# Gated linear attention into a cosine router: products of 64 by 64 on TensorE for scores and state outputs, pairs of outputs in two PSUM banks, a new order of the turnings

## The chip, the cores and the metric

One core of a Trainium2 chip. The metric is the device time of one execution in microseconds (us), the median of three runs; lower is better.

## The reference

Two layers, all in 32-bit floats. The first is a gated linear attention over 4 sequences (batch) of 768 positions, with 8 heads of width 48:

```
f = sigmoid(f_logit)
for t in range(768):
    state = f[t] * state + outer(k[t], v[t])      # one 48 x 48 state per sequence and head
    y[t]  = q[t] @ state
```

The outputs of the 8 heads side by side are 3072 rows x of width 384. The second layer sends each row to one of 8 experts, the one whose embedding is nearest to the row by cosine, and computes `gate * (relu(x @ w1[e]) @ w2[e])`, with w1 of 384 x 1024 and w2 of 1024 x 384.

## The kernel before, in words

The attention runs in 24 **steps**, each a chunk of 128 positions of one sequence (`steps`, L713: six chunks, in each the four sequences in turn). Within a chunk the recurrence is written as products of matrices. For step i:

- `decays` (ACT, L740) and `suffixes` (L748: one product on PE, a clip on DVE at L753, two exponentials on ACT) make the decay factors `ek` and `eq`.
- `keys` and `queries` (DVE, L788 and L799) scale k and q by them; `keys2` and `queries2` turn both on PE (`turn`, L734) and copy the turned tiles out of PSUM as `kz` (ACT) and `qa` (DVE). Two heads, a **pair** (hp), share the 128 partitions of such a tile, the even head in the lower half, the odd in the upper (par 0 and 1), each head padded from 48 to 64 rows.
- `scores` (L810) multiplies kz by qa, one product of 64 rows by 128 columns for each head, into two banks sc0 and sc1; `scores2` masks them on DVE into `am`.
- `whole` and `carry` (POOL, L760 and L769) take the decay of the whole chunk through a small DMA into `pc_all`, and multiply the old state of the sequence by it: `old`. `carried` (L780) copies `old` on ACT into `st`, a tile in which each head has 64 columns over all 128 partitions, zero in the half of the other head.
- `outputs` (L849) adds up for each head, in one bank `f_y`, a product with the old state (L859, 128 rows by 64 columns, `st`; none in the first chunk of a sequence) and one with the masked scores (L865). ACT copies the bank out as `xT` (L870).
- `update2` (L830) makes the new state (L838 on PE, an addition on DVE at L846). `rows_out` (L873) turns the outputs into rows and router logits with one product by `unit` for each pair (L881); `logits`, `route`, `count` and `place` rank the rows by expert, and `scatter` (POOL, L936) sends them to `x_sorted` in DRAM, sorted by expert.

The order of all instructions on each engine is as written. The first steps follow a list (`opening`, L1144), then a loop (L1170) runs for i from 4 to 22; in one turn of it PE gets: suffixes(i+2), keys2(i+1), queries2(i+1), rows_out(i-2), a ranking product in every second to fourth turn (`settle`), scores(i), outputs(i-1), update2(i). The loads of q, k, v and f_logit (L719, DMAs of 192 KB issued by SP) run six steps ahead, from L1171 on; the first expert's weights are issued behind the loads of i = 8. Some straight code then ends the last steps (L1191 to L1213), and starts the first expert with 256 of its rows (L1213 to L1247).

PSUM has eight banks. In the attention stage three are the rotating buffers `tp` (ps_t, taken in turn by suffixes, keys2 and queries2), and misc, small, sc0, sc1 and f_y take one each. The experts follow in a second part (L1250 on), bound by PE throughout, which the change doesn't touch.

Of the kernel before, what the change touches and what calls it, by code (L numbers as in the profile page):

```python
# [10 lines left out]
FP32 = mybir.dt.float32  # L11
# [563 lines left out]
def kernel(  # L575
# [25 lines left out]
    nc = tc.nc  # L601
# [33 lines left out]
    with ExitStack() as fast:  # L635
# [50 lines left out]
            wts[k] = w1, w2  # L686

        with tc.tile_pool(name="f_fix", bufs=1) as fix, tc.tile_pool(name="f_work", bufs=2) as work, tc.tile_pool(
            name="ps_t", bufs=3, space=PSUM
        ) as ps_t, tc.tile_pool(name="ps_s", bufs=1, space=PSUM) as ps_s:  # L690
            NLD = 6
            lds = {nm: [fix.tile([P, H, DH], FP32, name=f"f_{nm}{i}") for i in range(NLD)] for nm in "qkf"}
            NV = NLD + 2
            lds["v"] = [fix.tile([P, H, 64], FP32, name=f"f_v{i}") for i in range(NV)]
            NS = 2
            sts = [fix.tile([P, HP, 2, 64], FP32, name=f"st{i}") for i in range(NS)]
            halves = [slice(0, 64), slice(64, P)]
            misc = ps_s.tile([P, 512], FP32, name="misc")
            small = ps_s.tile([P, 512], FP32, name="small")
# [19 lines left out]
            def load(nm, i):  # L719
# [11 lines left out]
                if nm == "v":  # L731
                    live[i]["v"] = t

            def turn(src, pairs=range(HP)):  # L734
                ps = ps_t.tile([P, HP, P], FP32, name="tp", tag="tp")
                for hp in pairs:
                    nc.tensor.transpose(ps[:, hp], src[:, 2 * hp : 2 * hp + 2].rearrange("p h d -> p (h d)"), ident)  # L737
                return ps
# [8 lines left out]

            def suffixes(i):  # L748
                L = live[i]
                ps = ps_t.tile([P, HP, P], FP32, name="tp", tag="tp").rearrange("p n t -> p (n t)")[:, 0 : H * DH]  # L750
                nc.tensor.matmul(ps, lhsT=upon, rhs=L["lf"], start=True, stop=True)  # L751
                cl = work.tile([P, H * DH], FP32, name="f_cl", bufs=1)
                nc.vector.tensor_scalar(cl, ps, S_MAX, None, ALU.min)  # L753
                ek = work.tile([P, H, DH], FP32, name="f_ek", bufs=3)
                nc.scalar.activation(ek.rearrange("p h d -> p (h d)"), cl, AF.Exp, scale=-1.0)  # L755
                eq = work.tile([P, H, DH], FP32, name="f_eq", bufs=2)
                nc.scalar.activation(eq.rearrange("p h d -> p (h d)"), cl, AF.Exp)
                L["ek"], L["eq"] = ek, eq
# [10 lines left out]
            def carry(i):  # L769

                b, c = steps[i]
                if c == 0:
                    return
                old = work.tile([P, HP, DH], FP32, name="old", bufs=3)
                nc.gpsimd.tensor_tensor(  # L775
                    old, state[b], pc_all[:, i].unsqueeze(2).to_broadcast([P, HP, DH]), ALU.mult
                )
                live[i]["old"] = old

            def carried(i):  # L780
                if steps[i][1] == 0:
                    return
                st = sts[i % NS]
                for par, r in enumerate(halves):
                    nc.scalar.copy(st[r, :, par, 0:DH], live[i]["old"][r])
                live[i]["st"] = st

            def keys(i):  # L788
                L = live[i]
# [20 lines left out]
            def scores(i):  # L810
                L = live[i]
                kz, qa = L["kz"], L["qa"]
                sc = [ps_s.tile([P, HP, P], FP32, name=f"sc{par}") for par in range(2)]
                for hp in range(HP):
                    for par in range(2):
                        r = slice(64 * par, 64 * par + 64)
                        nc.tensor.matmul(sc[par][:, hp], lhsT=kz[r, hp], rhs=qa[r, hp], start=True, stop=True)  # L817
                L["sc"] = sc

            def scores2(i):  # L820
# [28 lines left out]
            def outputs(i):  # L849
                b, c = steps[i]  # L850
                L = live[i]
                if i == NST - 1:
                    y = ps_t.tile([P, HP, P], FP32, name="tp", tag="tp")
                else:
                    y = ps_s.tile([P, HP, P], FP32, name="f_y")
                if c:
                    for hp in range(HP):
                        for par, r in enumerate(halves):
                            nc.tensor.matmul(  # L859
                                y[r, hp], lhsT=L["st"][:, hp, par], rhs=L["qa"][:, hp],  # L860
                                start=hp == 0, stop=False, skip_group_check=True,
                            )
                for hp in range(HP):
                    for par, r in enumerate(halves):
                        nc.tensor.matmul(  # L865
                            y[r, hp], lhsT=L["v"][:, 2 * hp + par], rhs=L["am"][:, par, hp],
                            start=c == 0 and hp == 0, stop=True, skip_group_check=True,
                        )
                xT = work.tile([P, HP, P], FP32, name="f_xT")
                nc.scalar.copy(xT, y)  # L870
                L["xT"] = xT

            def rows_out(i):  # L873
                L = live[i]
                rows_ps = misc
                if i == NST - 1:
                    rows_ps = ps_t.tile([P, HP, P], FP32, name="tp", tag="tp").rearrange("p n t -> p (n t)")
                rows_ps = rows_ps[:, 0 : HP * RW].rearrange("p (n w) -> p n w", w=RW)
                L["rows"] = rows_ps
                for hp in range(HP):  # L880
                    nc.tensor.matmul(rows_ps[:, hp], lhsT=L["xT"][:, hp], rhs=unit[:, hp], start=True, stop=True)  # L881
                x4 = xg[(i // B) % 2]
                row = x4[:, i % B]
                if i % B == 0:
                    nc.scalar.copy(x4[:, :, C_TOK], tok[:, i : i + B])
                x = row[:, 0:D]
                nc.scalar.copy(x.rearrange("p (n w) -> p n w", n=HP), rows_ps[:, :, 0 : 2 * DH])
                sq = work.tile([P, D], FP32, name="f_sq", bufs=1)
                nc.scalar.activation(sq, x, AF.Square, accum_out=row[:, C_SSQ : C_SSQ + 1])
                L["row"] = row  # L890
# [73 lines left out]
            def first():  # L964
# [24 lines left out]
                nc.vector.memset(pc_all, 1.0)  # L989
                for t in lds["v"][1:]:  # L990
                    nc.gpsimd.memset(t[:, :, DH:64], 0.0)
                for t in sts:
                    nc.gpsimd.memset(t, 0.0)
                for t in xg:
                    nc.gpsimd.memset(t[:, :, D:R], 0.0)
# [2 lines left out]
            def norm(part):  # L998
# [3 lines left out]
                    nc.scalar.activation(esq, emb[:, :, 0:DH], AF.Square, accum_out=ss)  # L1002
                if part == 6:
                    for hp in range(HP):
                        nc.scalar.copy(unit[:, hp, 0 : 2 * DH].rearrange("p (r d) -> p r d", r=2), eyes)
                if part == 1:
                    nc.gpsimd.tensor_scalar(ss, ss, 1.0e-30, None, ALU.max)
                    nc.gpsimd.tensor_tensor(rroot, ss, rroot, ALU.pow)
# [13 lines left out]
            def units():  # L1022
                ps = misc[:, 0 : HP * E]
                for hp in range(HP):
                    nc.tensor.transpose(
                        ps[:, hp * E : hp * E + E],
                        emb[:, 2 * hp : 2 * hp + 2].rearrange("e h d -> e (h d)"),
                        ident[0:E, 0:E],
                    )
                nc.scalar.copy(unit[:, :, 2 * DH : RW], ps.rearrange("p (n e) -> p n e", e=E))  # L1030

            def prepare(part):
# [79 lines left out]
            def at(i, fn):  # L1112
                if 0 <= i < NST:
                    fn(i)
# [55 lines left out]
            for i in range(FROM, NST - 1):  # L1170
                loads(i)  # L1171
                at(i + 3, decays)
                at(i + 2, suffixes)
                at(i + 1, carry)
                at(i + 2, whole)
                at(i + 1, keys2)
                at(i + 1, queries2)
                at(i + 2, keys)
                at(i + 2, queries)
                at(i - 2, rows_out)  # L1180
                settle()
                at(i - 2, logits)
                send(1 if i < NST - 4 else 2)
                at(i, scores)
                at(i, scores2)
                at(i, carried)
                at(i - 1, outputs)
                finish(i - 2)
                at(i, update2)
                if i == FROM:  # L1190
                    prepare(2)  # L1191
            scores(NST - 1)
            scores2(NST - 1)
            carried(NST - 1)
            rows_out(NST - 3)
            settle()
            outputs(NST - 2)
# [12 lines left out]
            settle()  # L1210
            finish(NST - 1)
            send(B)
            xt = [ps_t.tile([P, 2, EARLY], FP32, name="tp", tag="tp") for _ in range(2)]  # L1213
            for c in range(DC):
                for j in range(2):
                    nc.tensor.transpose(xt[c // 2][:, c % 2, j * P : j * P + P], xs_a[:, j, c * P : c * P + P], ident)
# [7 lines left out]
            )  # L1224
            whose(1)
            for f in range(FC):
                ps = ps_t.tile([P, 2, EARLY], FP32, name="tp", tag="tp")[:, 0]
                for c in range(DC):
                    nc.tensor.matmul(  # L1229
                        ps, lhsT=wts[0][0][:, c, f * P : f * P + P], rhs=xT_0[:, c, 0:EARLY],  # L1230
# [7 lines left out]
                    check()  # L1238
                if f == 6:
                    checked()  # L1240
                    lt = [ps_t.tile([P, 2, 2, PL], FP32, name="tp", tag="tp", padded_shape=[P, 2, 2, P]) for _ in range(2)]
                    for c in range(DC):
                        for j in range(2):
                            nc.tensor.transpose(lt[c // 2][:, c % 2, j], xs_b[0:PL, j, c * P : c * P + P], ident[0:PL, 0:PL])
# [264 lines left out]
```

## Time and profile before

| what | value |
|---|---|
| median of three runs | 430.54 us (430.49 to 430.96) |
| the profiled execution, its own time | 428.34 us |
| span from its first to its last instruction | 426.6 us |
| PE busy | 417.0 us, 98% of the span |
| ACT, DVE, POOL busy | 46%, 62%, 55% |

The span ends 1.7 us short of the execution's own time. PE is TensorE's products, PEld its weight loads, DVE VectorE, ACT ScalarE, POOL GpSimd, SPq the queue that issues DMAs. Each product of 32-bit floats is two matmul instructions in the trace, so 8 heads are 16 matmuls.

### The profile page before, as it was taken

Reading aid. Unit: us, or ns where it says so; the run is one execution under the profiler, and the core shown is the slowest. Engines: PE = TensorE matmul, PEld = TensorE weight load, DVE = VectorE, ACT = ScalarE, POOL = GpSimd, SP = SyncE. Lnnn points to the kernel's source line nnn. Section 1 sums busy time; section 2 is a strip of 40 time slices with the busy share of each in tenths; the row PEclk is TensorE's granted clock in tenths of the full one; section 3 lists DMA queues with packets and bytes.
Section 4 is the critical chain, followed back from the end, with each engine's and each line's share of the span. In section 5 each row is a group of like instructions: output and inputs, shape, how many; then the busy total and the mean of one; then the engine's idle time right before and its main releaser. Section 6 shows DMA issues by size and latency. Waiting matters only on the chain.

```text
span 426.6 us, 9051 instructions
## 1 busy us (share of the span) xinstructions
PE 417.0 (98%) x3384; PEld 337.6 (79%) x3384; DVE 263.8 (62%) x673; ACT 198.2 (46%) x480; POOL 234.1 (55%) x265
## 2 busy tenths in 40 slices
PE   7999999999999999999999999999999999999994
PEld 5688989898989989659858957966966966967952
DVE  4778776677777434776765584595585585583500
ACT  7888787678776531242062063044134134144210
POOL 8535543564456337606764773886972963962111
PEclk9999999999999999999999999999999999999998
DMA  8999999899931327910380191093083083051011
GB/s 173 188 198 213 243 222 235 287 223 223 219 90 40 120 78 246 320 42 2 124 287 9 14 368 43 2 306 98 20 298 114 2 288 120 2 164 40 19 54 40
DMA packets 120480, 61.60 MB, mean 144 GB/s; under 512 B 104779, under 2 KB 114112, under 8 KB 120428
## 3 DMA queue, kind: packets, MB, share of 16 engines
q1 hardware_dynamic: 113612, 51.21, 45.3%
q0 software_dynamic: 6816, 9.73, 7.0%
q8 instruction: 29, 0.48, 0.5%
q14 instruction: 23, 0.19, 0.1%
HBM read 49.58 MB, written 11.63 MB: 143 GB/s over the span
## 4 chain that ended last, share of the span: by engine, by line
PE 84%; issue 8%; POOL 3%; SPq 2%; DMA 1%; DVE 1%; POOLq 1%; ACT 0%; DVEq 0%
PE h_ps L1311 25%; PE y_ps L1372 20%; PE sc L817 6%; PE f_y L865 5%; PE misc L881 5%; PE f_y L859 5%; PE tp L737 5%; PE tp L751 4%; PE tp L1229 2%; PE small L838 2%; POOL out_dram L1399 2%; PE x_tp L1272 2%; PE y_tp L1412 2%; SPq L730 1%; DMA f_q<-in_q_dram 1%
## 5 line engine op out<-in xcount | busy, mean ns | idle before, releaser
L1311 PE MATMUL h_ps<-xT,w 128*128 128x384 f32 (+6 forms) x384 | 130.8, 484 | 0.0
L1340 POOL TENSOR_TENSOR wsum<-w 128x512 f32<-128x512 f32 x63 | 78.9, 1279 | 53.9 <-PE y_ps L1372 48.8
L1311 PEld LDWEIGHTS h_ps<-xT,w 128*128 128x128 f32 x384 | 68.0, 190 | 38.7 <-issue 24.0
L1318 ACT ACTIVATE hT<-h_ps 128x384 f32<-128x384 f32 (+6 forms) x60 | 29.8, 497 | 129.3 <-PE h_ps L1311 129.3
L1383 DVE TENSOR_TENSOR yTs<-yTs,y_ps 128x147 f32<-128x147 f32 (+6 forms) x189 | 48.5, 296 | 53.8 <-ACT yTs L1385 26.8
L1399 POOL DMA_INDIRECT out_dram<-f_yo,gtok x30 | 42.6, 1420 | 47.1 <-ACT f_yo L1398 43.0
L1372 PE MATMUL y_ps<-hsum,wsum 128*128 128x147 f32 (+5 forms) x384 | 51.1, 283 | 0.0
L1340 DVE TENSOR_TENSOR hsum<-hT 128x588 f32<-128x588 f32 (+6 forms) x49 | 49.0, 1025 | 0.0
L1372 PEld LDWEIGHTS y_ps<-hsum,wsum 128*128 128x128 f32 x384 | 48.3, 189 | 0.0
L937 POOL DMA_INDIRECT x_sorted<-f_xg,f_pos_i x24 | 24.5, 1019 | 18.6 <-DVE hot L914 8.4
L825 DVE TENSOR_TENSOR am<-sc,causal 128x512 f32<-128x512 f32 x48 | 30.8, 683 | 3.9 <-PE sc L817 3.8
L762 POOL COPY f_pc<-f_ek 1x384 f32<-1x384 f32 x24 | 22.4, 934 | 19.5 <-ACT f_ek L755 18.8
L817 PE MATMUL sc<-qa,kz 64*128 64x128 f32 x384 | 27.9, 285 | 0.0
L1273 DVE COPY xT<-x_tp 128x384 f32<-128x384 f32 (+5 forms) x21 | 12.3, 584 | 24.7 <-PE x_tp L1272 24.4
L1385 ACT ACTIVATE yTs<-y_ps 128x147 f32<-128x147 f32 (+6 forms) x63 | 15.0, 286 | 25.6 <-DVE yTs L1383 15.0
L1372 PE MATMUL y_ps<-hT,wsum 128*128 128x147 f32 (+5 forms) x192 | 26.1, 283 | 0.0
L775 POOL TENSOR_TENSOR old<-new,pc_all 128x192 f32<-128x192 f32 x20 | 10.1, 504 | 28.8 <-DMA pc_all<-f_pc 27.5
L1340 POOL TENSOR_TENSOR wsum<-w,wsum 128x512 f32<-128x512 f32 x14 | 20.0, 1425 | 10.7 <-PE y_ps L1372 10.1
L817 PEld LDWEIGHTS sc<-qa,kz 64*128 64x128 f32 x384 | 23.3, 187 | 2.6 <-DVE am L825 0.5
L1372 PEld LDWEIGHTS y_ps<-hT,wsum 128*128 128x128 f32 x192 | 24.3, 189 | 0.0
L865 PE MATMUL f_y<-am,f_v 128*64 128x128 f32 x368 | 24.2, 274 | 0.0
L881 PE MATMUL misc<-unit,f_xT 128*128 128x104 f32 x184 | 24.1, 274 | 0.0
(194 smaller groups left out, 717.1 us busy)
## 6 DMA issues: line engine op xcount, KB each, us to landing
w<-in_moe_w_dram SPq DMA_DIRECT2D x16, 1536.0 KB, 10.7
f_k<-in_k_dram SPq DMA_DIRECT2D x24, 192.0 KB, 4.1
f_q<-in_q_dram SPq DMA_DIRECT2D x24, 192.0 KB, 4.1
f_v<-in_v_dram SPq DMA_DIRECT2D x24, 192.0 KB, 4.0
f_f<-in_f_logit_dram SPq DMA_DIRECT2D x20, 192.0 KB, 4.0
xs<-x_sorted SPq DMA_DIRECT2D x5, 700.0 KB, 9.0
x_sorted<-xs_b SPq DMA_DIRECT2D x1, 1600.0 KB, 8.5
xs<-x_sorted SPq DMA_DIRECT2D x2, 600.0 KB, 7.2
```

Of the source, the lines that this page charges most:

```text
L762: nc.gpsimd.tensor_copy(row[:, :, 0:DH].rearrange("o r d n -> o n r d"), live[i]["ek"][0:1].rearrange("o (n r) d -> o n r d", r=2))
L817: nc.tensor.matmul(sc[par][:, hp], lhsT=kz[r, hp], rhs=qa[r, hp], start=True, stop=True)
L825: nc.vector.tensor_tensor(am[:, par], sc[par], causal.unsqueeze(1).to_broadcast([P, HP, P]), ALU.mult)
L865: nc.tensor.matmul(y[r, hp], lhsT=L["v"][:, 2 * hp + par], rhs=L["am"][:, par, hp], start=c == 0 and hp == 0, stop=True, skip_group_check= ...
L881: nc.tensor.matmul(rows_ps[:, hp], lhsT=L["xT"][:, hp], rhs=unit[:, hp], start=True, stop=True)
L937: nc.gpsimd.indirect_dma_start(out=x_views[s][:], out_offset=bass.IndirectOffsetOnAxis(ap=pos_i[:, s : s + 1], axis=0), in_=live[s]["row"] ...
L1311: nc.tensor.matmul(ps, lhsT=w1[:, c, f * P : f * P + P], rhs=xTs[k][:, c, lo:cap], start=c == 0, stop=c == DC - 1,)
L1318: nc.scalar.activation(hTs[k][:, f, lo:cap], ps, AF.Relu)
L1340: engine.tensor_tensor(blocks[6 + i], blocks[one], blocks[other], ALU.add if sign > 0 else ALU.subtract)
L1372: nc.tensor.matmul(ps, lhsT=h if rows_first else w, rhs=w if rows_first else h, start=m == 0, stop=m == FC // 2 - 1,)
L1383: nc.vector.tensor_tensor(y, y, ps, ALU.add if sign > 0 else ALU.subtract)
L1399: nc.gpsimd.indirect_dma_start(out=out_views[k * NB + j][:], out_offset=bass.IndirectOffsetOnAxis(ap=gtok[0:n, k, j : j + 1], axis=0), in_ ...
```

## The change

It computes the same. Five things change in the attention stage:

1. `scores`: each head's product of 64 rows by 128 columns becomes two of 64 by 64, one for each half of the columns.
2. `outputs`: the product with the old state takes `old` itself (three tiles `olds`, padded to 64 columns), 64 rows by 64 columns, in place of the zero-padded `st`. `carried` and its two ACT copies a step go. The outputs of even pairs lie in bank f_y, those of odd pairs in a new bank f_y_odd, and there with the two heads' halves swapped; `xT` is copied out in two halves. The constants in `unit` are swapped to match.
3. `ps_t` has two buffers in place of three, since f_y_odd takes a bank. Until the first outputs, f_y_odd serves as a third turning bank (`bank`).
4. In the loop keys(i+2) and rows_out(i-2) come ahead of queries2(i+1).
5. At the end of the stage the banks sc0 and sc1 join the rotation.

```
-            name="ps_t", bufs=3, space=PSUM
+            name="ps_t", bufs=2, space=PSUM
...
-            NS = 2
-            sts = [fix.tile([P, HP, 2, 64], FP32, name=f"st{i}") for i in range(NS)]
+            olds = [fix.tile([P, HP, 64], FP32, name=f"old{i}") for i in range(3)]
...
+            stage = {"names": ["tp", "tp", "f_y_odd"], "n": 0}
+
+            def bank():
+                nm = stage["names"][stage["n"] % len(stage["names"])]
+                stage["n"] += 1
+                if nm == "tp":
+                    return ps_t.tile([P, HP, P], FP32, name="tp", tag="tp")
+                return ps_s.tile([P, HP, P], FP32, name=nm)
...
-                old = work.tile([P, HP, DH], FP32, name="old", bufs=3)
+                old = olds[i % len(olds)][:, :, 0:DH]
...
-            def carried(i):
-                if steps[i][1] == 0:
-                    return
-                st = sts[i % NS]
-                for par, r in enumerate(halves):
-                    nc.scalar.copy(st[r, :, par, 0:DH], live[i]["old"][r])
-                live[i]["st"] = st
...
-                        nc.tensor.matmul(sc[par][:, hp], lhsT=kz[r, hp], rhs=qa[r, hp], start=True, stop=True)
+                        for h in halves:
+                            nc.tensor.matmul(
+                                sc[par][h, hp], lhsT=kz[r, hp, h], rhs=qa[r, hp], start=True, stop=True,
+                                skip_group_check=True,
+                            )
...
-                    y = ps_s.tile([P, HP, P], FP32, name="f_y")
+                    stage["names"] = ["tp"]
+                    ys = [ps_s.tile([P, HP, P], FP32, name=nm)[:, 0 : HP // 2] for nm in ("f_y", "f_y_odd")]
+                heads = [(hp, par) for hp in range(HP) for par in range(2)]
+
+                def place_of(hp, par):
+                    return ys[hp % 2][halves[(par + hp) % 2], hp // 2]
+
                 if c:
-                    for hp in range(HP):
-                        for par, r in enumerate(halves):
-                            nc.tensor.matmul(
-                                y[r, hp], lhsT=L["st"][:, hp, par], rhs=L["qa"][:, hp],
-                                start=hp == 0, stop=False, skip_group_check=True,
-                            )
...
+                    for hp, par in heads:
+                        r = halves[par]
                         nc.tensor.matmul(
+                            place_of(hp, par), lhsT=olds[i % len(olds)][r, hp], rhs=L["qa"][r, hp],
+                            start=hp < 2, stop=False, skip_group_check=True,
                         )
...
-                nc.scalar.copy(xT, y)
+                for z in range(2):
+                    nc.scalar.copy(xT.rearrange("p (n z) t -> p z n t", z=2)[:, z], ys[z])
...
                 at(i + 1, keys2)
+                at(i + 2, keys)
+                at(i - 2, rows_out)
                 at(i + 1, queries2)
-                at(i + 2, keys)
                 at(i + 2, queries)
-                at(i - 2, rows_out)
...
                 at(i, scores2)
-                at(i, carried)
                 at(i - 1, outputs)
```

## Rows read from the trace of the kernel before

**Rows 1.** The page: the span, and PE's busy time, share and instructions.

```profile
span 426.6 us, 9051 instructions
PE 417.0 (98%) x3384; PEld 337.6 (79%) x3384; DVE 263.8 (62%) x673; ACT 198.2 (46%) x480; POOL 234.1 (55%) x265
```

**Rows 2.** The chain of waits, one turn of the loop: start us, us, what.

```profile
105.40 1.09 PE sc L817 x16
106.49 1.02 PE f_y L859 x16
107.51 0.87 PE f_y L865 x16
108.39 0.45 PE small L838 x16
108.84 0.84 PE tp L751 x2
109.68 0.87 PE tp L737 x8
110.55 0.87 PE misc L881 x8
```

**Rows 3.** Groups by line and form on PE, whole run.

```profile
L817 PE MATMUL sc<-qa,kz 64*128 64x128 f32 x384 | 27.9, 285 | 0.0
...
L859 PE MATMUL f_y<-qa,st 128*64 128x128 f32 x304 | 20.8, 279 | 0.0
...
L859 PE MATMUL tp<-qa,st 128*64 128x128 f32 x16 | 1.0, 273 | 0.0
```

**Rows 4.** Chain of waits, the outputs of the last two steps (columns as in 2).

```profile
146.26 1.02 PE f_y L859 x16
...
148.16 0.87 PE tp L859 x16
```

**Rows 5.** Busy time by engine in one stretch: matmuls, granted clock (PEclk), DMA.

```profile
118.00:122.00 4.00, 4.00 (x67) 3.51 (x66) 2.55 (x8) 2.52 (x7) 1.63 (x2) 1.00 0.64 152
```

**Rows 6.** Groups by line on ACT: us, mean ns | idle before, releaser.

```profile
L785 ACT COPY st<-old 64x192 f32<-64x192 f32 x40 | 13.7, 342 | 0.3
...
L870 ACT COPY f_xT<-f_y 128x512 f32<-128x512 f32 x23 | 13.4, 583 | 21.6 <-PE f_y L865 21.6
```

**Rows 7.** Timeline of SP's queue: start us, us of issue.

```profile
68.87 0.70 SPq L683 DMA_DIRECT2D w<-in_moe_w_dram  x1
...
70.93 9.64 SPq L728 DMA_DIRECT2D f_f<-in_f_logit_dram  x1
...
85.34 0.75 SPq L728 DMA_DIRECT2D f_f<-in_f_logit_dram  x1
```

**Rows 8.** Timeline of ACT behind that load: start us, us, what [idle before, releaser].

```profile
85.36 0.52 ACT L743 ACTIVATE f_u<-f_f 128x384 f32<-128x384 f32 x1 [0.84 <-DMA f_f<-in_f_logit_dram]
...
86.34 0.51 ACT L755 ACTIVATE f_ek<-f_cl 128x384 f32<-128x384 f32 x1
...
88.67 0.69 ACT L785 COPY st<-old 64x192 f32<-64x192 f32 x2
```

**Rows 9.** Timeline of DVE in the same stretch.

```profile
86.09 0.69 DVE L807 COPY qa<-tp 128x512 f32<-128x512 f32 x1 [0.32 <-PE tp L737]
86.88 0.78 DVE L791 TENSOR_TENSOR f_kt<-f_k,f_ek 128x384 f32<-128x384 f32 x1
...
90.48 0.35 DVE L846 TENSOR_TENSOR new<-old,small 128x192 f32<-128x192 f32 x1
91.24 0.56 DVE L753 TENSOR_SCALAR f_cl<-tp 128x384 f32<-128x384 f32 x1 [0.41 <-PE tp L751]
92.12 0.69 DVE L807 COPY qa<-tp 128x512 f32<-128x512 f32 x1 [0.32 <-PE tp L737]
```

**Rows 10.** Timeline of POOL, one round of the chunk's decay.

```profile
104.87 0.89 POOL L762 COPY f_pc<-f_ek 1x384 f32<-1x384 f32 x1 [0.55 <-ACT f_ek L755]
106.06 0.59 POOL L765 DMA_DIRECT2D pc_all<-f_pc  x1 [0.30 <-POOL f_pc L762]
...
108.98 0.50 POOL L775 TENSOR_TENSOR old<-new,pc_all 128x192 f32<-128x192 f32 x1 [1.00 <-DMA pc_all<-f_pc]
```

More of the change, by code (lines that the diff above doesn't have):

```diff
@@ L732, in load @@
                     live[i]["v"] = t
+            stage = {"names": ["tp", "tp", "f_y_odd"], "n": 0}
[5 more added lines that the diff above has]
+                return ps_s.tile([P, HP, P], FP32, name=nm)
             def turn(src, pairs=range(HP)):
-                ps = ps_t.tile([P, HP, P], FP32, name="tp", tag="tp")
+                ps = bank()
                 for hp in pairs:
@@ L749, in suffixes @@
                 L = live[i]
-                ps = ps_t.tile([P, HP, P], FP32, name="tp", tag="tp").rearrange("p n t -> p (n t)")[:, 0 : H * DH]
+                ps = bank().rearrange("p n t -> p (n t)")[:, 0 : H * DH]
                 nc.tensor.matmul(ps, lhsT=upon, rhs=L["lf"], start=True, stop=True)
@@ L852, in outputs @@
                 if i == NST - 1:
-                    y = ps_t.tile([P, HP, P], FP32, name="tp", tag="tp")
+                    ys = [bank()[:, 0 : HP // 2] for _ in range(2)]
                 else:
-                    y = ps_s.tile([P, HP, P], FP32, name="f_y")
-                if c:
-                    for hp in range(HP):
-                        for par, r in enumerate(halves):
-                            nc.tensor.matmul(
-                                y[r, hp], lhsT=L["st"][:, hp, par], rhs=L["qa"][:, hp],
-                                start=hp == 0, stop=False, skip_group_check=True,
-                            )
-                for hp in range(HP):
-                    for par, r in enumerate(halves):
+                    stage["names"] = ["tp"]
[3 more added lines that the diff above has]
+                    return ys[hp % 2][halves[(par + hp) % 2], hp // 2]
+                if c:
+                    for hp, par in heads:
+                        r = halves[par]
                         nc.tensor.matmul(
-                            y[r, hp], lhsT=L["v"][:, 2 * hp + par], rhs=L["am"][:, par, hp],
-                            start=c == 0 and hp == 0, stop=True, skip_group_check=True,
-                        )
+                            place_of(hp, par), lhsT=olds[i % len(olds)][r, hp], rhs=L["qa"][r, hp],
+                            start=hp < 2, stop=False, skip_group_check=True,
+                        )
+                for hp, par in heads:
+                    nc.tensor.matmul(
+                        place_of(hp, par), lhsT=L["v"][:, 2 * hp + par], rhs=L["am"][:, par, hp],
+                        start=c == 0 and hp < 2, stop=True, skip_group_check=True,
+                    )
                 xT = work.tile([P, HP, P], FP32, name="f_xT")
-                nc.scalar.copy(xT, y)
+                for z in range(2):
+                    nc.scalar.copy(xT.rearrange("p (n z) t -> p z n t", z=2)[:, z], ys[z])
                 L["xT"] = xT
@@ L876, in rows_out @@
                 if i == NST - 1:
-                    rows_ps = ps_t.tile([P, HP, P], FP32, name="tp", tag="tp").rearrange("p n t -> p (n t)")
+                    rows_ps = ps_s.tile([P, HP, P], FP32, name="sc0").rearrange("p n t -> p (n t)")
                 rows_ps = rows_ps[:, 0 : HP * RW].rearrange("p (n w) -> p n w", w=RW)
@@ L991, in first @@
                     nc.gpsimd.memset(t[:, :, DH:64], 0.0)
-                for t in sts:
+                for t in olds:
                     nc.gpsimd.memset(t, 0.0)
@@ L1004, in norm @@
                     for hp in range(HP):
-                        nc.scalar.copy(unit[:, hp, 0 : 2 * DH].rearrange("p (r d) -> p r d", r=2), eyes)
+                        to = unit[:, hp, 0 : 2 * DH].rearrange("p (r d) -> p r d", r=2)
+                        if hp % 2:
+                            for r in range(2):
+                                nc.vector.tensor_copy(to[:, r], eyes[:, 1 - r])
+                        else:
+                            nc.scalar.copy(to, eyes)
                 if part == 1:
@@ L1024, in units @@
                 for hp in range(HP):
[L1025 to L1029, printed above, removed]
+                    to = ps[:, hp * E : hp * E + E]
+                    if hp % 2:
+                        for r in range(2):
+                            nc.tensor.matmul(
+                                to[halves[1 - r]], lhsT=emb[:, 2 * hp + r], rhs=ident[0:E, 0:E], start=True, stop=True
+                            )
+                    else:
+                        nc.tensor.transpose(
+                            to, emb[:, 2 * hp : 2 * hp + 2].rearrange("e h d -> e (h d)"), ident[0:E, 0:E]
+                        )
                 nc.scalar.copy(unit[:, :, 2 * DH : RW], ps.rearrange("p (n e) -> p n e", e=E))
@@ L1193 @@
             scores2(NST - 1)
-            carried(NST - 1)
             rows_out(NST - 3)
@@ L1212 @@
             send(B)
-            xt = [ps_t.tile([P, 2, EARLY], FP32, name="tp", tag="tp") for _ in range(2)]
+            stage.update(names=["tp", "tp", "sc1", "sc0"], n=0)
+            xt = [bank().rearrange("p n t -> p (n t)").rearrange("p (n t) -> p n t", n=2) for _ in range(2)]
             for c in range(DC):
@@ L1226 @@
             for f in range(FC):
-                ps = ps_t.tile([P, 2, EARLY], FP32, name="tp", tag="tp")[:, 0]
+                ps = bank().rearrange("p n t -> p (n t)")[:, 0:EARLY]
                 for c in range(DC):
@@ L1240 @@
                     checked()
-                    lt = [ps_t.tile([P, 2, 2, PL], FP32, name="tp", tag="tp", padded_shape=[P, 2, 2, P]) for _ in range(2)]
+                    lt = [bank().rearrange("p (n j) t -> p n j t", j=2)[:, :, :, 0:PL] for _ in range(2)]
                     for c in range(DC):
```

## The prediction

> **What bounds the kernel.** I began with the page: PE is busy for 417.0 of 426.6 us [rows 1], so a change pays only if PE's own work shrinks, and only where nothing else then ends last. Next came the chain of waits. Through one turn of the attention loop it runs on PE alone, seven groups end to end: 1.09 + 1.02 + 0.87 + 0.45 + 0.84 + 0.87 + 0.87 = 6.01 us, with no other engine between [rows 2]. The groups by form say how often each comes: the scores 384/16 = 24 times, the products with the old state (304 + 16)/16 = 20 times, 18 of them in the loop and two in the closing code [rows 3]. The granted clock is 1.00, the 2.4 GHz level, with PE busy throughout [rows 5]; the stage afterwards has no pause, so I price nothing for the clock.
>
> The reader should see in rows 2 what a small tile is worth. The rows products (8 matmuls, whole array) take 109 ns each. The masked-score products at L865, 128 by 64, take 0.87/16 = 54 ns though their moving operand is wider (128 against 104 columns): two of them, on the two halves of the columns, run at once. The scores (64 by 128) and L859 are also at two at once, with 0.22 and 0.15 us on top of 0.87; each of the two is the first group after a change of the tile's form, so I take these as the price of that change. L838, 128 by 64 too, takes 0.45/16 = 28 ns with 48 moving columns, so PE can be handed a matmul and its weights every 28 ns.
>
> **The change, part by part.**
>
> Old state. A product of 64 by 64 uses a quarter of the array, and the four neighbours in the new order lie on four different quarters. Four at once should start every 109/4 = 27 ns, 16 in 0.44 us. The bounds are 27 ns (four at once) and 54 ns (two, as L865); I take 27, since L838's 28 ns shows that the feeding allows it and nothing in rows 2 makes two tiles disturb each other.
>
> Scores. 32 products of a quarter in place of 16 of a half: 32 x 27 = 0.87, plus the 0.22 for the change of form, 1.09 as before. At 54 ns they would take 1.96.
>
> Change of form. Scores and old state now share one form, so the 0.15 moves from L859 to L865, which becomes 1.02; their number stays three a turn. The turn: 1.09 + 0.44 + 1.02 against 1.09 + 1.02 + 0.87, **0.43 us less**. In the loop 18 x 0.43 = 7.7. At the end, outputs stand between groups of other forms: step 22 goes from 1.02 + 0.87 to 0.59 + 1.02 (0.28 less), step 23 from 0.87 + 0.87 to 0.59 + 1.02 (0.13 less) [rows 4]. Sum 8.1 us.
>
> ACT. The two copies of `st` go (0.69 a step). The copy of `xT` becomes two of half its width: between 0.34 each (the 64x192 copy) and 0.58 (the full one), on the line between them 0.39, so 0.78 for 0.58 [rows 6]. ACT gets some 0.5 us lighter, worth nothing by itself, as it waits for PE at L870 anyway. The cover for the later end of `xT` is 0.45 + 0.84 + 0.43 us of PE work ahead of the next rows products; the copies need 0.8. No cost in an ordinary turn.
>
> Two turning banks, keys and rows_out moved. Queries2 now needs the bank of the suffixes of the same turn, that is, the clip at L753 must have read it. Between the two PE has keys2 (0.43) and the rows (0.87), 1.3 us; in rows 9 the clip ends 0.56 us after it starts, about 0.4 behind the suffixes. On DVE, the copy of `qa` is queued behind keys, which waits for ACT's `ek`. In an ordinary turn that fits. No DMA is moved; POOL's order stays.
>
> POOL. Its round is copy, DMA, product: 108.98 + 0.50 - 104.87 = 4.6 us [rows 10], below the new turn of 5.58, so it isn't the next bound.
>
> Opening. Three banks until the first outputs, as before; `unit` and the fixed tiles change by a few tenths in both directions. I take 0, bounds ±0.5 (half an `xT` copy a step on either side).
>
> **What is late next: one load.** The weights of the first expert are issued at 68.87; the load of f_logit behind them sits 9.64 us in the issue, and ACT starts on it at 85.36, already 0.84 us late [rows 7, 8]. The loads are issued one behind the other, held by the DMAs and not by PE, so a faster PE doesn't move this. Before, the lateness had cover. By this turn (i = 13) PE will have gained 8 x 0.43 = 3.4 us. Then: ACT's `ek` of this turn still ends near 86.85, and DVE has keys queued there, now with `qa` behind it. Before, DVE ran from keys (86.88) to the state addition (90.48) without a pause, 3.60 us; add the `qa` copy 0.69, that addition 0.35 and the next clip 0.56: the clip ends near 92.0 [rows 9]. Queries2 of turn 14 needs that bank. Before, it began near 91.6 (its copy at 92.12 less 0.5); it would now be due at 91.6 + 0.87 (rows moved ahead) - 9 x 0.43 = 88.6. PE so stands up to 3.4 us. Overlap of neighbouring DVE instructions can take some off: I take **3.2 us given back**, bounds 1 and 3.5. Later loads come every 4 us, so it happens once.
>
> Net: 8.1 - 3.2 = 4.9 us. The profiled execution, 428.34 with its span of 426.6, would become 423.4; it lies 2.2 below the median, so the forecast of the median is 430.54 - 4.9 = **425.6 us**. After the stage all is bound by PE or follows it, and shifts as a whole.
>
> **Against a page.** The rows of L865 overlap although all of them use all 128 rows of the array. The Trainium skill ("TensorE: Matmul & The Clock Gate", Part 3, What overlaps and what doesn't) says that a weight load overlaps a running matmul only where the row group differs. By it neighbouring 64 by 64 tiles on the same rows would gain nothing over two at once, and the time would be that of the first rival below; L865's 54 ns speaks against it.
>
> **Rivals.**
>
> *Only two tiles at once* (slower). Place: L817. Price: scores 0.22 + 32 x 54 ns = 1.96, +0.87 in each of 24 steps; the old state 0.87, its 0.15 moved on: no gain. +20.9 us, median 451.4. It decides from 36 ns a product on, where 0.22 + 48 x 36 ns + 1.02 equals the old 2.98. For it: no row shows four at once. Against: L838 and L865. 10%, with milder cases between 37 and 54 ns.
>
> *PE is short of instructions* (no change). A turn has 82 matmuls and would have 98; the densest 4 us I found hold 67, 60 ns each [rows 5]. At 60 ns, 98 take 5.88 us: 0.13 gained a turn, 2.4 in all, less 0 to 1 given back: about 428.5. The same page (Part 1) says that PE's sequencer, if it decodes in software, spends about 62 ns on a matmul; by that a turn would be 6.08 us and the time about 432. L838's runs of 28 ns are too short to exclude this. 10%.
>
> *The late load costs nothing* (PE's gain whole): if the DMAs, with fewer scatters in their way or a better turn, bring it 3 us sooner, 430.54 - 8.1 = 422.4. Against it: it was late already. 15%.
>
> *The two banks cost in every turn*: if queries2 waits some 0.2 us for the clip, 18 x 0.2 = 3.6, and 429.2. For it: DVE now blocks on `ek`. Against: the 1.3 us of cover. 10%.
>
> **How the numbers follow.** The forecast, 425.6 with 3.2 given or 1 to 3.5, spans 423.4 to 426 and holds 55%. The range has to take in the whole gain plus 0.5 of the opening, 421.9, and the milder bank rival, up to 429.2; beyond it lie the slower rival and part of the second, about 2 in 10. A run can be told from no change by about 0.2%, 0.9 us. Faster 0.82, same 0.07, slower 0.11.
>
> **What would show it.** The chain's turn near 5.6 us; L817 near 1.09 with 32 matmuls and the old state's 16 in 0.44; L865 up to 1.02. ACT idle some 4 us before the exponential at 85 us, and PE idle near 89 to 92. Wrong if L817 is near 2 us, or if PE's idle time is spread over all turns.

## The result and the profile after

| | before | changed | ratio [95%] |
|---|---|---|---|
| median, us | 430.68 (430.49 to 430.96) | 423.33 (422.56 to 423.63) | 0.9826 [0.9809, 0.9843] |
| profiled execution, us | 428.34 | 423.18 | |
| its span, us | 426.6 | 421.5 | |

Faster by 1.7%. The range (421.9 to 429.2) holds the time; the forecast, 425.6, was 2.3 us too high. The profiled executions differ by 5.2 us (4.9 forecast), the medians by 7.35.

The page of the changed kernel, its span and PE's line, to be read against [rows 1]:

```profile
span 421.5 us, 9811 instructions
PE 408.4 (97%) x3774; PEld 325.2 (77%) x3774; DVE 258.5 (61%) x677; ACT 186.3 (44%) x462; POOL 237.8 (56%) x266
```

PE lost 8.6 us of work, with 390 more matmuls in the record (384 of them the scores'), and still bounds the kernel; but it now stands idle for 13.1 us of the span, where it stood for 9.6.

The chain of waits through one turn of the changed kernel (start us, us, what), to be read against [rows 2]; the left-out lines are the other small steps of the old state between 103.25 and 103.69:

```profile
102.22 1.03 PE sc L818 x32
103.25 0.09 PE f_y L869
103.34 0.01 PE f_y_odd L869 x2
...
103.69 0.37 PE f_y L874 x4
104.06 0.22 PE f_y_odd L874 x4
104.28 0.22 PE f_y L874 x4
104.49 0.22 PE f_y_odd L874 x4
104.71 0.45 PE small L842 x16
105.16 0.84 PE tp L759 x2
106.01 0.44 PE tp L745 x4
106.44 0.87 PE misc L891 x8
107.32 0.44 PE tp L745 x4
107.75 1.03 PE sc L818 x32
```

The old state takes 103.69 - 103.25 = 0.44 us instead of 1.02, the scores 1.03 instead of 1.09, the masked scores 0.37 + 3 x 0.22 = 1.03 instead of 0.87. The rest is as it was, and no other engine stands between: 5.53 us from scores to scores, where it was 6.03 by the same reckoning.

Now the one turn that isn't like this. The timeline of SP's queue, ACT, DVE and PE around the late load of f_logit (start us, us, engine, what [idle before, releaser]), to be read against [rows 7 to 9]:

```profile
71.95 7.22 SPq L727 DMA_DIRECT2D f_f<-in_f_logit_dram  x1
...
84.02 0.52 ACT L751 ACTIVATE f_u<-f_f 128x384 f32<-128x384 f32 x1 [3.66 <-DMA f_f<-in_f_logit_dram]
...
85.54 0.84 DVE L791 TENSOR_TENSOR f_kt<-f_k,f_ek 128x384 f32<-128x384 f32 x1 [3.77 <-ACT f_ek L763]
86.30 0.68 DVE L807 COPY qa<-tp 128x512 f32<-128x512 f32 x1
...
87.47 1.27 DVE L829 TENSOR_TENSOR am<-sc,causal 128x512 f32<-128x512 f32 x2
...
89.52 0.55 DVE L761 TENSOR_SCALAR f_cl<-tp 128x384 f32<-128x384 f32 x1
...
82.85 1.10 PE L818 MATMUL sc<-qa,kz 64*64 64x128 f32 x32
...
86.44 0.91 PE L759 MATMUL tp<-f_lf,f_upon 128*128 128x384 f32 x2 [0.32 <-ACT kz L796]
...
90.12 0.66 PE L745 MATMUL tp<-f_ident,f_qt 128*128 128x128 f32 x4 [1.21 <-DVE f_cl L761]
...
91.08 1.10 PE L818 MATMUL sc<-qa,kz 64*64 64x128 f32 x32
```

The load lies 7.22 us in the issue behind the first expert's weights, and ACT waits 3.66 us for it. DVE then works without a pause from keys (85.54) to the clip (89.52), and PE stands before queries2 until the clip has read its bank. Scores to scores take 91.08 - 82.85 = 8.23 us instead of 5.90 (a turn with the ranking's products in it): 2.33 lost. PE stands twice, the first time (0.32) before the suffixes, whose bank ACT had yet to empty into `kz`. Counted from start to start, the two stands take 0.39 and 1.52 us more than the same steps of an undisturbed turn (late_w below), and small delays the rest.

**Where the 5.2 us of the span come from**, by the lead over the kernel before at five points: 0.0 us at the scores of step 5 (37.84, before 37.85); 6.7 at those of step 23 (137.33, before 144.03: eighteen turns at 0.50 are 9.0, less 2.33); 6.1 at the first expert's first product (148.44, before 154.54); 5.4 at the first output product of the experts (188.44, before 193.81); 5.2 at the end. So the code behind the loop loses 0.6 and the first expert another 0.7. Rows on PE show where:

```profile
137.33 1.22 PE L818 MATMUL sc<-qa,kz 64*64 64x128 f32 x20
138.83 0.67 PE L818 MATMUL sc<-qa,kz 64*64 64x128 f32 x12 [0.28 <-issue]
...
160.47 5.88 PE L1330 MATMUL h_ps<-xT,w 128*128 128x184 f32 x36 [0.52 <-DVE hT L1253]
```

The scores of step 23 took 2.17 us instead of 1.10, with a pause that the profile shows no cause for. And where the first expert's early products went into `tp` banks alone, `sc` now takes turns with them, and PE waits 0.52 for DVE to empty one. The wait is the same, 0.52, in the profiles of all the versions of the changed kernel below, and in neither of the kernel before; that the banks cause it is read from their names, not tried.

### The profile page after: what moved, and what is told of

Read it like the earlier page. It is cut to its first block, busy times and chain, and to the rows that moved or that the text cites. A ratio compares the mean times of both kernels' runs of the same rounds, so it can differ in the third digit from the quotient of the medians.

```text
span 421.5 us, 9811 instructions
## 1 busy us (share of the span) xinstructions
PE 408.4 (97%) x3774; PEld 325.2 (77%) x3774; DVE 258.5 (61%) x677; ACT 186.3 (44%) x462; POOL 237.8 (56%) x266
## 4 chain that ended last, share of the span: by engine, by line
PE 80%; issue 9%; DMA 4%; POOL 3%; ACT 1%; DVE 1%; SPq 1%; POOLq 1%; ACTq 0%; DVEq 0%
PE h_ps L1330 26%; PE y_ps L1391 21%; PE sc L818 5%; PE misc L891 4%; PE tp L745 4%; DMA f_f<-in_f_logit_dram 4%; PE tp L759 4%; PE f_y L874 3%; POOL out_dram L1418 2%; PE f_y_odd L874 2%; PE small L842 2%; PE x_tp L1291 2%; PE sc L1248 2%; PE y_tp L1431 2%; PE f_y L869 1%
## 5 line engine op out<-in xcount | busy, mean ns | idle before, releaser
L770 POOL COPY f_pc<-f_ek 1x384 f32<-1x384 f32 x24 | 26.1, 1088 | 8.8 <-ACT f_ek L763 7.7
L818 PE MATMUL sc<-qa,kz 64*64 64x128 f32 x768 | 27.2, 276 | 0.4 <-issue 0.3
L791 DVE TENSOR_TENSOR f_kt<-f_k,f_ek 128x384 f32<-128x384 f32 x24 | 14.3, 596 | 16.7 <-ACT f_ek L763 15.4
L818 PEld LDWEIGHTS sc<-qa,kz 64*64 64x64 f32 x768 | 20.9, 132 | 4.3 <-issue 3.4
```

The source lines that it names most:

```text
L770: nc.gpsimd.tensor_copy(row[:, :, 0:DH].rearrange("o r d n -> o n r d"), live[i]["ek"][0:1].rearrange("o (n r) d -> o n r d", r=2))
L818: nc.tensor.matmul(sc[par][h, hp], lhsT=kz[r, hp, h], rhs=qa[r, hp], start=True, stop=True, skip_group_check=True,)
```

## The experiments

All are the changed kernel or edits of it but one, which is the kernel before. They ran in three sets, each on one chip beside the kernel before: after_again, late_w, old_order and sc_half where that took 430.26 us, late_w_2, w12, rows_apart and before_again where it took 428.92, the other four where it took 430.9. So a time is read by its ratio. A turn is scores to scores in the profile.

### What the turn is made of

**sc_half**: the scores as before, 16 products of 64 by 128.

```
-                        for h in halves:
-                            nc.tensor.matmul(
-                                sc[par][h, hp], lhsT=kz[r, hp, h], rhs=qa[r, hp], start=True, stop=True,
-                                skip_group_check=True,
-                            )
+                        nc.tensor.matmul(sc[par][:, hp], lhsT=kz[r, hp], rhs=qa[r, hp], start=True, stop=True)
```

> Against the changed kernel, only the scores are products of 64 by 128 again. Theory (32 quarters cost what 16 halves cost, but the same form as the state products saves a change of form, and the quarter form starts cheaper): the scores group goes from 1.03 to 1.09 us and the state group from 0.44 to about 0.59, 0.2 us a turn, some 4.0 us in 20 steps: 427.3. Rival (the scores in quarters are worth more, because four at once hide the weight loads): the scores group 1.2 or more, and 429 or more. Rival (they are worth nothing): 423.3.

427.0 us, ratio 0.9927 [0.9913, 0.9941], and a turn of 5.75. Its chain of waits, from the scores to the masked scores:

```profile
103.81 1.09 PE sc L817 x16
104.90 0.26 PE f_y L865 x2
...
105.50 0.37 PE f_y L870 x4
```

The scores take 1.09 again, and the old state 105.50 - 104.90 = 0.60 instead of 0.44. The masked scores begin with 0.37 as in the changed kernel, so this version pays for one change of form more. Four at once thus brings the scores themselves nothing (they were two at once, of twice the size); quartering them saves the 0.16 of that change, and 0.06 on their own first product: 0.22 x 18 = 4.0 us of the gain. The medians of this set differ by 3.6, but that is no second proof: this profile has no long turn where the load of f_logit comes (6.12 there, an ordinary turn with the ranking's products), and loses 1.0 and 0.8 us in two other turns. The rest, 0.28 a turn, is the old state, which had been padded to twice its rows.

**rows_apart**: the order of the score products alone, so that neighbours use the same 64 rows.

```
-                for hp in range(HP):
-                    for par in range(2):
+                for par in range(2):
+                    for hp in range(HP):
```

> Against the changed kernel, the scores' products are issued with all of the even heads (upper 64 rows) first and then all of the odd heads, so that neighbours share their rows and differ only in their columns. Theory (tiles on different columns run side by side though they share rows, two at once, 54 ns a product): the scores group takes 32 x 54 ns and its start, 1.9 us in place of 1.03, 24 x 0.87 = 21 us more, 444 us. Rival (a weight load overlaps only with products on other rows): 32 x (27 + 107) ns = 4.3 us a group, some 500 us. Rival (the order doesn't matter): 423.3.

431.31 us in its one execution, where the kernel before took 428.92: the whole gain gone. A turn takes 6.02. PE's timeline at the end of the scores (start us, us):

```profile
108.61 0.32 PE L869 MATMUL f_y<-qa,old 64*64 64x128 f32 x1
108.71 0.28 PE L818 MATMUL sc<-qa,kz 64*64 64x128 f32 x2
108.78 0.27 PE L869 MATMUL f_y<-qa,old 64*64 64x128 f32 x1
108.82 0.28 PE L818 MATMUL sc<-qa,kz 64*64 64x128 f32 x2
108.83 0.32 PE L869 MATMUL f_y_odd<-qa,old 64*64 64x128 f32 x1
108.88 0.28 PE L869 MATMUL f_y<-qa,old 64*64 64x128 f32 x1
108.93 0.28 PE L818 MATMUL sc<-qa,kz 64*64 64x128 f32 x2
```

The scores on one half of the rows come two in 0.11 us, some 54 ns each, which is two at once. All the same the turn grows by less than the 0.87 us more that 32 scores at 54 ns would take: state products (L869), later in the program, start ahead of the last scores, which by the program's order use the other half of the rows. So the order of neighbours is worth 0.49 us a turn, and what waits is a tile of the array, not PE as a whole.

**old_order**: two banks, but the order of steps as before.

```
+                at(i + 1, queries2)
                 at(i + 2, keys)
-                at(i - 2, rows_out)
-                at(i + 1, queries2)
                 at(i + 2, queries)
+                at(i - 2, rows_out)
```

> Against the changed kernel, the turn's order is that of the kernel before again (keys2, queries2, keys, queries, rows_out), with two turning banks kept. Theory (the rows products cover the clip that must free the bank for queries2): after the suffixes PE has only keys2, 0.44 us, until queries2, and the clip ends about 0.75 us after the suffixes; PE stands some 0.35 us in each of 19 turns, 6.6 us, and the time is about 430. Rival (the cover isn't needed, the clip is quick enough): 423.3.

431.33 us, 1.0036 [1.0017, 1.0055]: slower than the kernel before. A turn takes 5.97. Its chain between the suffixes and the next scores:

```profile
102.94 0.85 PE tp L759 x2
...
103.82 0.57 DVE f_cl L761
...
104.43 0.66 PE tp L745 x4
105.09 0.87 PE misc L891 x8
105.96 1.03 PE sc L818 x32
```

DVE's clip stands in PE's chain: 0.44 us in each turn. The rows products between are what makes two banks enough: keys_late below, which puts keys alone back behind queries2 and leaves the rows products ahead, keeps its ordinary turns at 5.53.

### The late load

**after_again** and **after_3**: the changed kernel itself, on two more chips.

> The changed kernel once more, beside the others of this call, so that they can be compared on one chip. My theory (PE's turn 0.49 us shorter, some 2.4 us given back behind the late load of f_logit): 423.3 us again, a turn of 5.53 us. If part of the gain in the median came from the executions of the kernel before and not from the change, its ratio to the kernel before moves from 0.983 towards 0.988 (the two profiled executions: 423.18 / 428.34).

> The changed kernel a third time, as the measure for the three beside it: a ratio of 0.983 to the kernel before, a long turn of some 8.2 us behind the late load of f_logit, and in some executions 1 to 2 us more where the clock falls or a copy waits for a scatter.

423.36 us, 0.9838 [0.9826, 0.9851], and 425.88, 0.9877 [0.9846, 0.9907]. The profiled executions were among the longest, 425.27 and 427.86. ACT waited 3.89 and 6.04 us for the load; scores to scores took 8.41 and then 7.15, in after_3 11.12 and then 7.06. After_3's rows on ACT and PE:

```profile
86.67 0.53 ACT L751 ACTIVATE f_u<-f_f 128x384 f32<-128x384 f32 x1 [6.04 <-DMA f_f<-in_f_logit_dram]
...
89.10 0.91 PE L759 MATMUL tp<-f_lf,f_upon 128*128 128x384 f32 x2 [2.86 <-ACT kz L796]
...
94.24 1.99 PE L818 MATMUL sc<-qa,kz 64*64 64x128 f32 x32
```

and its busy time by stretch (length, PE, PEld, DVE, ACT, POOL with instructions in brackets, granted clock, DMA share, GB/s):

```profile
84.00:88.00 4.00, 2.24 (x57) 1.94 (x48) 0.00 (x0) 1.30 (x3) 0.56 (x2) 1.00 0.80 178
88.00:92.00 4.00, 2.90 (x14) 2.41 (x14) 3.74 (x11) 2.82 (x10) 2.90 (x3) 0.83 1.04 201
92.00:96.00 4.00, 3.78 (x42) 3.46 (x45) 2.47 (x7) 3.41 (x9) 2.47 (x4) 0.50 1.11 242
96.00:100.00 4.00, 4.00 (x62) 3.30 (x56) 1.99 (x4) 1.60 (x4) 1.33 (x2) 0.81 0.94 206
```

PE is busy for little more than half of 84 to 88 us; the granted clock then falls to 0.50, its 1.2 GHz level, and the same 32 scores take 1.99 instead of 1.10 us. The load therefore costs 2.3 us in the first profile, 2.5 + 1.6 in after_again and 5.2 + 1.5 in after_3.

The wait goes with the speed of the turn. In sc_half, old_order and rows_apart the weights stand at the same place, but a turn takes 5.75 to 6.02 us, and ACT waits 0.25 us for this load or not at all. Sc_half's row:

```profile
82.82 0.52 ACT L751 ACTIVATE f_u<-f_f 128x384 f32<-128x384 f32 x1 [0.25 <-DMA f_f<-in_f_logit_dram]
```

**late_w**, and again as **late_w_2** on another chip: the first expert's weights issued behind the stage's last loads instead of at step 8.

```
-                if i == 8:
+                if i == NST - NLD - 1:
```

> Against the changed kernel, only the issue of the first expert's weights is moved behind the last loads of q, k, v and f_logit (from i = 8 to i = 17). Theory (the late load is what gives back part of the gain): the exponential no longer waits 3.66 us for its load, PE's two pauses before it turn the tiles of step 14 and 15 go, the turn around 85 us takes 5.9 us instead of 8.2, and the time falls by 2.3 us to 421.0. Rival (the loads are slow with or without the weights, or the two banks are what stops PE there): 423.3, a pause stays. Other rival: the weights then come too late for the first expert at 148 us, and the time rises by what is missing.

> The same kernel as late_w, to see why its times spread from 421.6 to 427.5 while its profile of 421.6 shows no pause. Theory (a spell of the lower clock after a short pause, as in the second profile of the changed kernel, 0.57 from 92 to 96 us): executions near 421.6 at a clock of 1.00, and slower ones with a stretch well below it. Rival (the weights at 109 us collide with something in some executions): a wait for a DMA in the slow ones.

424.1 us, 0.9873 [0.9834, 0.9913], and 421.43, 0.9838 [0.9812, 0.9864]. Both profiles (421.64 and 419.95) have no long turn. But the times spread, 421.64 to 427.46 in the first, and none of the longer executions was profiled: what they lost isn't known. In its median late_w isn't faster than the changed kernel beside it (after_again, 423.36).

**w12**: the same with `i == 12`.

> Against the changed kernel, the first expert's weights are issued behind the loads of i = 12 in place of 8. Theory (loads gain some 1.3 us of lead a turn, 5.53 us a turn against 4.2 a step's loads; four turns give 5.2 us, more than the 3.66 us that the load was late): no wait for f_logit, the long turn gone, 2.3 us less than the changed kernel in its undisturbed executions, 421.0. Rival (any flood of weights stops the loads for 12 us, and lead doesn't help): 423.3.

422.48 us, 0.9855 [0.9839, 0.9871]; here the longest was profiled, 426.36. It doesn't wait for f_logit; two turns, 9.34 and 7.29, are long behind another transfer. The first of them on ACT and PE:

```profile
72.10 0.20 ACT L895 COPY f_xg<-f_tok 128x4 f32<-128x4 f32 x1 [4.67 <-DMA x_sorted<-f_xg,f_pos_i]
...
73.63 1.82 PE L891 MATMUL misc<-unit,f_xT 128*128 128x104 f32 x8 [2.44 <-ACT f_xT L880]
```

ACT's copy of the tokens needs a buffer `xg` that a scatter still reads, and `xT` is queued behind it on ACT. Behind this pause, too, the granted clock falls (0.75 from 72 to 76 us), and the next scores take 1.65. So there are two transfers that a faster PE can catch up with.

**xg3** and **late_xg3**: three such buffers, on the changed kernel and with late_w's edit.

```
-            xg = [fix.tile([P, B, R], FP32, name=f"f_xg{i}") for i in range(2)]
+            xg = [fix.tile([P, B, R], FP32, name=f"f_xg{i}") for i in range(3)]
-                x4 = xg[(i // B) % 2]
+                x4 = xg[(i // B) % len(xg)]
-                lg = xg[(s0 // B) % 2][:, s0 % B : s0 % B + n, C_LG : C_LG + E]
+                lg = xg[(s0 // B) % len(xg)][:, s0 % B : s0 % B + n, C_LG : C_LG + E]
```

> Against the changed kernel, three buffers of rows (xg) in place of two, so that ACT's copy of the token numbers need not wait for the scatters of eight steps before. Theory (that wait, 1.3 to 4.7 us in the profiles seen, is a second place where the shorter turn has used up the slack, and the spread of the times comes from it): the waits for x_sorted on ACT are gone, the median is 0.3 to 1 us lower, the long turn of 8.2 us stays. Rival (PE never waits for that copy, its cover suffices): no change, the same spread.

> Against the changed kernel, the weights behind the last loads (as in late_w) and three buffers of rows. Theory: both places where the shorter turn ran out of slack are gone, all turns take 5.53 or 5.90 us, the time is 2.5 to 3 us below the changed kernel in the same call, and the spread of late_w (421.6 to 427.5) is gone. Rival (the spread has another cause): the same spread as late_w.

xg3: 425.83 us, 0.9892 [0.9878, 0.9907], no better than after_3 in the same set. ACT's waits for scatters are gone, the long turn (10.15) is there. late_xg3: 422.95 us (421.71 to 424.13), 0.9824 [0.9805, 0.9843], 2.9 us under after_3 beside it, with intervals that just don't overlap. Three scores groups in a row on PE, where the long turn had been:

```profile
83.63 1.10 PE L818 MATMUL sc<-qa,kz 64*64 64x128 f32 x32
...
89.53 1.10 PE L818 MATMUL sc<-qa,kz 64*64 64x128 f32 x32
...
95.07 1.10 PE L818 MATMUL sc<-qa,kz 64*64 64x128 f32 x32
```

5.90 and 5.54 us: no trace of the late load. It beats the three other versions of its set, and its times spread over 2.4 us instead of late_w's 5.8, on another chip.

So the long turn is in all five profiles that have the weights at step 8 and a turn of 5.53 (the changed kernel's three, xg3, keys_late), and in none of the four with the weights moved. The medians say less: 0.9824 to 0.9873 with the weights moved, 0.9826, 0.9838 and 0.9877 for the changed kernel, and of the two versions that stand beside it in a set only late_xg3 is faster.

**keys_late**: keys behind queries2, so that what DVE does for queries2 isn't queued behind its wait for `ek`.

```
-                at(i + 2, keys)
                 at(i - 2, rows_out)
                 at(i + 1, queries2)
+                at(i + 2, keys)
```

> Against the changed kernel, keys(i+2) comes behind queries2(i+1) again, so that DVE copies qa before it waits for ek; rows_out stays ahead of queries2. My step (the copy of qa is queued behind keys in the stretch of the late load and adds its 0.6 us to the chain up to the clip that frees the bank): PE's long turn is 0.6 us shorter, other turns stay 5.53, the time falls by 0.6. Rival (in ordinary turns DVE then waits for queries2 with keys behind it, and the clip or the additions come later): the turns grow, and the time rises.

427.9 us (424.77 to 431.74), 0.9934 [0.991, 0.9958]: worse than after_3. With about the first profile's lateness (ACT waits 3.60) the long turn took 7.79 instead of 8.23, so by these two profiles the blocked queue is worth some 0.4 of it. But three later turns took 7.12, 6.22 and 6.34 (in the first profile 5.53, 5.08 and 4.74), the first of them so on ACT and PE:

```profile
117.94 0.20 ACT L895 COPY f_xg<-f_tok 128x4 f32<-128x4 f32 x1 [3.50 <-DMA x_sorted<-f_xg,f_pos_i]
...
119.47 1.19 PE L891 MATMUL misc<-unit,f_xT 128*128 128x104 f32 x8 [1.00 <-ACT f_xT L880]
```

Whether this order makes the scatters late or met them by chance, one profile doesn't tell.

### The kernel before, once more

**before_again**: to see whether its median hides a pause that its profile (2.2 us below) didn't have.

> The kernel before once more, with a profile. The first profiled execution took 428.34 us, the timed ones 430.3. Theory: the 2 us are a pause or a spell of the lower clock behind the late load of f_logit, which some executions have and the first profile had not; this one then takes about 430.3, and the turn near 85 to 95 us is longer than 6.42. Rival: they lie in the experts' part or at the ends, and the attention's turns are 6.03 and 6.42 as before.

428.82 us, on a chip where its median is 428.92; its turns are 6.03 and 6.41 as in the first profile, but for one of 6.41 instead of 6.03. So a profile at 428.3 need not be a lucky execution: on this chip that is near the ordinary time, and the medians of the three chips differ by 2 us (428.92, 430.26, 430.9). On which chip the first profile was taken isn't known, and what the kernel loses where it takes 430.3 to 430.9 was never profiled.

## Why the prediction was right, and where it was not

**Old state: right.** 16 products in 0.44 us, 27 ns each, four at once.

**Scores and change of form: right, with 0.06 mis-sized.** I kept 0.22 for the scores' change of form; 1.03 - 0.87 is 0.16. The 0.15 did move on to the masked scores (1.03; 1.02 forecast), and in sc_half, where the old state's form differs from both neighbours', it is paid on either side. With 0.06 more a turn, 0.43 became 0.50, and 7.7 became 9.0.

**ACT: right.** The two `xT` copies take 0.35 and 0.37 us, overlapped to 0.62 from start to end (0.78 forecast), and cost no ordinary turn anything.

**Two banks, rows between: right.** No ordinary turn has a wait for a bank, and old_order, without the rows between, has one in each. What I missed is the suffixes: they too take a bank, and wait for `kz` when ACT is late (0.32 in the first profile, 2.86 in after_3).

**Opening: right** (0.0; other profiles with this opening reach step 5 from 0.1 us earlier to 0.65 later). **Closing: the gain right, a pause in front of it not foreseen.** The profile loses 0.6 there instead of gaining 0.41. In w12 the scores of step 23 have no pause:

```profile
141.77 1.10 PE L818 MATMUL sc<-qa,kz 64*64 64x128 f32 x32
```

From there to the first expert's first product w12 takes 10.04 us, the kernel before 10.51 and the changed kernel's first profile 11.11. So 0.47 is gained without the pause, and the 1.07 between the two is what the scores took longer (2.17 against 1.10). The pause is in five of the profiles and not in late_w_2, w12, xg3 or after_again; what makes it stays open.

**"After the stage all shifts as a whole": wrong** by 0.7 in the first expert, and 0.2 after it. I hadn't followed the banks into the first expert's early products, where PE now waits 0.52 for `hT`.

**The late load: the mechanism right, its size not.** ACT's wait (some 4 us forecast, 3.66), the clip behind DVE's queue and PE's stand before queries2 came as described. For the first profile 3.2 was too much, 2.33 measured: the load left the queue at 71.95 + 7.22 = 79.17 us, 1.4 earlier than in [rows 7], and I had taken it as fixed. In after_again and after_3 it cost 4.1 and 6.7, above the bound of 3.5: the wait can be longer, and I priced nothing for the clock, since PE had no pause before; in these two the clock fell behind the pauses that I had forecast.

**Sum.** 9.0 - 2.33 - 0.6 - 0.7, less 0.2 after it, is the 5.2 of the span; that 8.1 - 3.2 = 4.9 came so close is luck, as errors in both directions cancelled. The forecast of the median missed by 2.3, since I hung the profile's gain on a median 2.2 us above it: the profile of before stands near the level of a chip at 428.9, the runs at 430.5 to 430.7, where the gain was 7.35. In the two later sets that hold the changed kernel it was 6.9 and 5.0. What the kernel before loses at 430.5, and the changed one doesn't, is open.

**The rivals.** *Two tiles at once* is out, by the 27 ns; rows_apart shows when it would be true. The Trainium skill's rule ("TensorE: Matmul & The Clock Gate", Part 3, What overlaps and what doesn't), that a weight load overlaps a running matmul only where the row group differs, doesn't describe these traces: on the same rows two products a column half apart still come at 54 ns each. *Short of instructions* is out: 48 in a row came in 1.47 us, 31 ns each with a change of form, where this rival needs 60. *The late load costs nothing* is wrong for this kernel. Its time, 422.4, is a ratio of 0.981; the experiments that moved the weights came to 0.9824 to 0.9873. *Two banks cost in every turn* is out here, and is old_order's result.

## What to carry to other kernels

Products on different quarters of TensorE's array run at once when neighbours in the program lie on different quarters; this pays where a product had been padded to a larger tile, and by grouping products of one form, so count changes of form as well as matmuls. When the bounding engine gets faster, list the transfers that arrive by their own clock: each one's slack shrinks with every turn, so move the large transfer behind the small ones it holds up, and see which transfer is late next. Fewer PSUM banks cost nothing if other work of the same engine stands between filling a bank and needing it again.

## What was not expected of the hardware

Products start out of the program's order when their part of the array is free: in rows_apart the products of L869 at 108.61, 108.78, 108.83 and 108.88 start ahead of scores (108.93) that stand before them in the program.

The granted clock fell to 0.50 behind a pause of PE of 2.86 us in after_3. In w12 it fell behind one of 2.44 (0.75 from 72 to 76 us), and in after_again behind two of 0.79 and 1.16 (0.57 from 92 to 96 us). In xg3, with pauses of 2.3 and 1.2, it didn't, nor in the first profile with 0.32 and 1.21. What decides that isn't settled.
